# Attention scores in row and column tiles, turns on VectorE and a state softmax that stays in SBUF

## The chip, the cores and the metric

The kernel runs on one core of a Trainium2 chip. The time is that of the device, in microseconds (us), as the median of timed runs. TensorE (PE in the rows) multiplies, with its weight loads shown as PEld; VectorE is DVE, ScalarE ACT, GpSimd POOL. SyncE (SP) issues the transfers.

## The reference

There are 4 batch entries with 8 heads, 512 tokens, 32 states and 64 columns a head. Tokens read the states and states read the tokens, each through a softmax of the same scores; the result, 544 rows for each entry and 512 columns, goes through two feed-forward layers of width 2048.

```python
scores = scale * np.matmul(x, state.transpose(0, 1, 3, 2))
a = softmax(scores)                     # over the 32 states
xread = np.matmul(a, state)
scores2 = scale * np.matmul(state, x.transpose(0, 1, 3, 2))
a2 = softmax(scores2)                   # over the 512 tokens
sread = np.matmul(a2, x)
x = concatenate([xread, sread], axis=2) # tokens to 2176 x 512 rows
h = x @ w_in;  g = elu(h);   x = g @ w_out
h = x @ w_in2; g = mish(h);  out = g @ w_out2
```

(The softmaxes are written out in the reference, with the maximum taken off and 1e-9 added to the sum. The weights arrive as 64-bit floats and are turned into 32-bit ones by the kernel.)

## The kernel before, in words

The token part of the attention is folded into the first layer: since xread is a times the states, xread @ w_in is a times (states @ w_in). `fold` makes those products ("m" tiles, 128 x 512 for four slices of w_in), and `token_reads` makes the probabilities ("x" tiles) for one entry b and one half hf of its heads. The first layer then runs in steps (b, j): a hidden product "h" of 128 slices of w_in by 512 tokens, the activation on ScalarE and VectorE ("e", "g" or "gw"), and the product with a slice of w_out into four PSUM banks ("acc"). The order of the steps is FIRST: entry 0 with j = 0 to 7, entry 1 with j = 0 to 7, entry 0 with 8 to 15, and so on; the states' own rows go through in between, and the second layer follows in five blocks of up to 512 tokens. Steps 0 to 7 of entry 0 use 32-bit products directly ("whole" w_out tiles for the first six); the others are split into a high and a low part, three products each.

`token_reads` loads x (xb), turns it on TensorE (xT), and multiplies it with `sd`, which holds the turned states of one entry in a block-diagonal form: for two token columns of 64 rows each, the states stand in one half and zeros in the other. The scores come out with tokens on the partitions. VectorE takes maximum, difference, sum and product over groups of 32, ScalarE the exponential, and four TensorE turns (pT) bring the probabilities into the form of x1. A copy of the raw scores (raw) goes to DRAM (s2d). `state_reads` fetches them back, and fetches x again in a form with a column of ones; it takes the maximum over the four token columns on VectorE and over the partitions on GpSimd, subtracts, takes the exponential, and multiplies (sr).

Each weight slice is loaded (raw_in, raw_out), decoded by ScalarE (wy) and three VectorE operations (wv, wv, w or whole), and split where the high and low parts are needed. The tiles of w_out take 16 slots called w_out, which also hold early temporaries; those of w_in and m take 16 slots called w_in.

Nothing of the order is left to the run. A planner (`Plan`) is given every operation with its engines, a cost, its due time and the buffers that it needs, and writes each engine's queue; an engine then works its queue strictly in that order. Operations given to either of ScalarE and VectorE are placed by the planner too.

Of the kernel before, what the change touches and what calls it, by code (L numbers as in the profile page):

```python
# [22 lines left out]
P = 128  # L23
# [17 lines left out]
class Buf:  # L41
# [7 lines left out]
    def __getitem__(self, i):  # L49
        return self.t[i]  # L50

# [5 lines left out]
class Plan:  # L57
# [59 lines left out]
    def run(self, take, dma):  # L117

        self.dues(dma)
        free = {}  # L120
# [15 lines left out]
        while todo:  # L136
# [52 lines left out]
            c = op.cost[e] if isinstance(op.cost, dict) else op.cost  # L189
            if e in dma:  # L190
# [25 lines left out]
def attention_elu_mish(  # L216
# [42 lines left out]
    s2d = pools["dram"].tile([P, B, 2, NC, P], F32, name="s2d")  # L259
# [77 lines left out]
    add("DVE", 2.8, make_ident, w=["ident"], due=-50.0)  # L337
# [4 lines left out]
    banks = itertools.cycle(["att", "acc0", "att", "acc1", "h", "acc2", "h"] + ([] if FILL else ["acc3"]))  # L342
    early = True

    def bank(name):
        tag = next(banks) if early else "att"
        return buf("ps", tag, 2 if tag in ("h", "att") else 1, [P, MAXN], F32, name)
# [16 lines left out]
    sd = [pools["at"].tile([P, 2, HH, 2, NS], F32, name=f"sd{b}") for b in range(B)]  # L364
# [11 lines left out]
    def load_states():  # L376
        raw = buf("w", "w_out", NF, [P, 2 * B, 2, D], F32, "st_raw")
        for i in range(2):
            A(ACTQ, 128.0, lambda i=i: nc.scalar.dma_start(
                out=raw[:, :, i, :], in_=state.rearrange("b (g h) n d -> (h n) (b g) d", g=2)),  # L380
              w=[(raw, i)], due=-50.0)
        for b in range(B):
            A("POOL", 0.5, lambda b=b: nc.gpsimd.memset(sd[b], 0.0), w=[("sd", b, i) for i in range(2)], due=-50.0 + b)
        st_raw.append(raw)

    def states(b0, b1):

        raw = st_raw[0]
        if True:
# [8 lines left out]
            for b in range(b0, b1):  # L398
                for i in range(2):
                    r = slice(i * D, (i + 1) * D)  # L400
                    A(EITHER, {"ACT": 0.41, "DVE": 0.43}, lambda e, b=b, b0=b0, i=i, r=r, pt=pt: copy(
                        e, sd[b][r, :, :, i, :],
                        pt[r, (b - b0) * 2 * P:(b - b0 + 1) * 2 * P].rearrange("p (g h n) -> p g h n", g=2, n=NS)),
                        r=[pt], w=[("sd", b, i)])
# [4 lines left out]
    def place_w1(j, k):  # L409
        return w1[j // 2].t.rearrange("p (k f) -> p k f", k=NK)[:, k, j % 2 * P:(j % 2 + 1) * P]  # L410
# [3 lines left out]
    def weight(kind, layer, j, due=None):  # L414
# [45 lines left out]
        if kind == "in" and layer == 1:  # L460
            if j // 2 not in w1:
                w1[j // 2] = buf("w", "w_in", NF, [P, NK * 2 * P], F32, f"w1_{j // 2}_")
            to = w1[j // 2]

            def sign():
                o = to.t.bitcast(U32).rearrange("p (k f) -> p k f", k=NK)[:, :, j % 2 * P:(j % 2 + 1) * P]
# [3 lines left out]
            add("DVE", 0.69, sign, r=[y, v], w=[(to, j % 2)])  # L470
            return
        if layer == 1 and j < WHOLE_OUT:
            w = w_sb["whole", layer, j] = buf("w", f"w_{kind}", NF, [P, DM], F32, f"whole{j}_")
# [12 lines left out]
    after_step = {}  # L486

    def split_weight(kind, layer, j, v):
        w = w_sb[kind, layer, j] = buf("w", f"w_{kind}", NF, [P, 2, DM], F32R, f"w_{kind}{layer}_{j}_")
        add(EITHER, {"ACT": 0.61, "DVE": 0.43}, lambda e: copy(e, w[:, 0, :], v.t), r=[v], w=[(w, 0)])  # L490
        lo, cost = (nc.gpsimd, {"POOL": 1.3}) if (kind, layer, j) in POOL_LO else (nc.vector, {"DVE": 0.69})
        add(next(iter(cost)), cost, lambda: lo.tensor_tensor(
            w[:, 1, :], v.t, w[:, 0, :].bitcast(F32), ALU.subtract), r=[v, (w, 0)], w=[(w, 1)])
# [10 lines left out]
    def m_tile(b, c):  # L504
        if (b, c) not in m_sb:
            m_sb[b, c] = buf("w", "w_in", NF, [P, 2, DM], F32, f"m{b}_{c}_")
        return m_sb[b, c]

    def fold(b, j0, j1):
# [5 lines left out]
        step = min(2, j1 - j0)  # L515

        def f(j):
            w = w1[j // 2].t.rearrange("p (k f) -> p k f", k=NK)
            c = slice(j % 2 * P, (j % 2 + step) * P)
            for k in range(NK):  # L520
                for e in range(2):
                    r, l = slice(e * D, (e + 1) * D), slice(k * NS, (k + 1) * NS)
                    nc.tensor.matmul(pts[e][l, (j - j0) * P:(j - j0 + step) * P], lhsT=sd[b][r, e, k, e, :],  # L523
                                     rhs=w[r, k, c], start=True, stop=True, tile_position=(e * D, k * NS))

        for j in range(j0, j1, step):
            A("PE", 0.1 + mm(4 * step * P), lambda j=j: f(j), w=[(pt, j) for pt in pts], place=[m, *pts],
              lag=FOLD_AHEAD if (b, j0) == (STATES_AFTER[0], STATES_AFTER[1] + 1) else FOLD_LAG,
              r=[("sd", b, 0), ("sd", b, 1)] + [(w1[i // 2], i % 2) for i in range(j, j + step)])
# [19 lines left out]
    x1, own = {}, {}  # L549

    def load_x(b, hf, due=None):

        t = buf("at", "xb", XB, [P, HH, NC, D], F32, "xb")
# [5 lines left out]
        return t  # L559

    def load_x_ones(b, hf):

        t = buf("at", "xb", XB, [P, NC, HH, D + 1], F32, "xb1_")
        A("POOL", 0.1, lambda: nc.gpsimd.memset(t[:, :, :, D:], 1.0), w=[(t, HH)])
        for h in range(HH):
            A(SP, 128.0 * X_WEIGHT, lambda h=h: nc.sync.dma_start(
                out=t[:, :, h, :D],
                in_=x[b, hf * HH + h].rearrange("(p c) d -> p c d", c=NC)), w=[(t, h)], lag=1.0)
        return t

    def token_reads(b, hf):
# [7 lines left out]
        if early and hf:  # L579
            xT = buf("w", "w_out", NF, [P, 2, S], F32, "xT")  # L580
            prr = buf("w", "w_out", NF, [P, 2, NC, P], F32, "prob")
            pr, raw = (lambda: prr[:, 0]), (lambda: prr[:, 1])
            kp, kr = (prr, 0), (prr, 1)
            held = [prr]
        else:
            xT = buf("at", "xT", 1, [P, 2, S], F32)
            kp, kr = buf("at", "prob", 1, [P, NC, P], F32), buf("at", "raw", 1, [P, NC, P], F32)
            pr, raw = (lambda: kp.t), (lambda: kr.t)
            held = [kp, kr]
        mx = buf("at", "mx", 2, [P, NC * HH])  # L590
        sm = buf("at", "sm", 2, [P, NC * HH])
        held += [mx, sm]
        lag = 0.0 if early else 1.0
        ahead = TOKENS_AHEAD[b]
        for q in range(2):
            pt = bank("xT")
# [9 lines left out]
        if b >= TILES_FROM:  # L606

            ps = [bank("scoresT") for t in range(2)]
            sTt = buf("at", "raw", 1, [P, NC, P], F32, "sT")
# [453 lines left out]
```

## Time and profile before

| what | value |
|---|---|
| timed runs, median (lowest, highest) | 753.81 us (752.93, 754.55) |
| profiled execution, first to last instruction (span) | 751.1 us |
| what the median lies above that span | 2.7 us |
| TensorE busy | 732.6 us, 98% |
| VectorE busy | 556.8 us, 74% |
| ScalarE busy | 425.0 us, 57% |
| GpSimd busy | 10.6 us, 1% |
| moved by transfers | 81.71 MB |

The page gives no other time for the profiled execution than its span. The engines run side by side, so their busy times are not to be added; what counts is which of them is never idle, in which stretch, and what ends its waits.

### The profile page before, as it was taken

Reading aid. Unit: us, or ns where it says so; the run is one execution under the profiler, and the core shown is the slowest. Engines: PE = TensorE matmul, PEld = TensorE weight load, DVE = VectorE, ACT = ScalarE, POOL = GpSimd, SP = SyncE. Lnnn points to the kernel's source line nnn. Section 1 sums busy time; section 2 is a strip of 40 time slices with the busy share of each in tenths; the row PEclk is TensorE's granted clock in tenths of the full one; section 3 lists DMA queues with packets and bytes.
Section 4 is the critical chain, followed back from the end, with each engine's and each line's share of the span. In section 5 each row is a group of like instructions: output and inputs, shape, how many; then the busy total and the mean of one; then the engine's idle time right before and its main releaser. Section 6 shows DMA issues by size and latency. Waiting matters only on the chain.

```text
span 751.1 us, 11051 instructions
## 1 busy us (share of the span) xinstructions
PE 732.6 (98%) x4098; PEld 598.0 (80%) x4098; DVE 556.8 (74%) x1048; ACT 425.0 (57%) x759; POOL 10.6 (1%) x27
## 2 busy tenths in 40 slices
PE   5899999999999999999999999999999999999996
PEld 5346677788777879878888888888889999999995
DVE  6988899988689895798999856565567565756564
ACT  3674767655567663577657445454455455545443
POOL 1000000010000000000000000000000000000000
PEclk8899999999999999999999999999999999999999
DMA  9953667453585543665845103000030020001001
GB/s 227 291 154 101 166 161 215 117 169 113 147 256 175 189 140 104 189 196 185 283 162 193 42 1 99 0 1 1 0 99 1 1 83 2 1 1 42 1 1 42
DMA packets 67292, 81.71 MB, mean 109 GB/s; under 512 B 22696, under 2 KB 45992, under 8 KB 67240
## 3 DMA queue, kind: packets, MB, share of 16 engines
q1 hardware_dynamic: 65028, 80.36, 36.1%
q10 hardware_dynamic: 2212, 0.66, 0.4%
q8 instruction: 32, 0.52, 0.3%
q14 instruction: 20, 0.16, 0.1%
HBM read 59.51 MB, written 21.50 MB: 108 GB/s over the span
## 4 chain that ended last, share of the span: by engine, by line
PE 94%; DMA 2%; DVE 1%; ACT 1%; issue 0%; SPq 0%; ACTq 0%
PE acc_acc L849 16%; PE acc_acc L851 15%; PE acc_acc L850 15%; PE h L769 12%; PE h L771 12%; PE h L770 12%; PE fold L523 2%; PE acc_acc L837 2%; PE h L745 2%; PE h L755 2%; DMA raw_in<-in_moe_w_in 2%; PE scores L638 1%; PE pT L663 1%; PE sr L697 1%; DMA xb<-in_x 1%; PE xT L600 1%
## 5 line engine op out<-in xcount | busy, mean ns | idle before, releaser
L788 ACT ACTIVATE e<-h 128x512 f32<-128x512 f32 (+1 forms) x148 | 83.2, 562 | 118.2 <-PE h L771 106.5
L813 ACT CAST g<-e 128x512 fp32r<-128x512 f32 (+1 forms) x142 | 82.4, 581 | 61.9 <-PE acc_acc L851 25.6
L771 PE MATMUL h<-x,w_in 128*128 128x384 f32 (+1 forms) x320 | 114.6, 358 | 0.0
L769 PE MATMUL h<-x,w_in 128*128 128x384 f32 (+1 forms) x320 | 114.4, 358 | 0.0
L770 PE MATMUL h<-x,w_in 128*128 128x384 f32 (+1 forms) x320 | 114.3, 357 | 0.0
L814 DVE TENSOR_TENSOR g<-e,g 128x512 fp32r<-128x512 f32 (+1 forms) x142 | 91.1, 642 | 22.5 <-ACT g L813 21.7
L851 PE MATMUL acc_acc<-w_out,g 128*128 128x512 f32 x272 | 106.9, 393 | 0.0
L850 PE MATMUL acc_acc<-w_out,g 128*128 128x512 f32 x272 | 106.7, 392 | 0.0
L849 PE MATMUL acc_acc<-w_out,g 128*128 128x512 f32 x272 | 105.9, 389 | 0.4 <-ACT g L813 0.4
L849 PE MATMUL acc_acc<-g,w_out 128*128 128x512 f32 x232 | 93.3, 402 | 0.0
L810 DVE TENSOR_TENSOR u<-u,e 128x384 f32<-128x384 f32 (+1 forms) x80 | 48.9, 611 | 57.7 <-ACT e L809 57.6
L850 PE MATMUL acc_acc<-g,w_out 128*128 128x512 f32 x232 | 90.5, 390 | 0.0
L851 PE MATMUL acc_acc<-g,w_out 128*128 128x512 f32 x232 | 90.5, 390 | 0.0
L808 ACT ACTIVATE e<-u,two 128x384 f32<-128x384 f32 (+1 forms) x80 | 52.8, 660 | 50.1 <-DVE u L806 49.9
L805 DVE TENSOR_SCALAR e<-e 128x384 f32<-128x384 f32 (+1 forms) x80 | 30.9, 387 | 48.2 <-ACT e L788 48.1
L769 PEld LDWEIGHTS h<-x,w_in 128*128 128x128 f32 x320 | 60.1, 188 | 7.1
L770 PEld LDWEIGHTS h<-x,w_in 128*128 128x128 f32 x320 | 60.1, 188 | 7.1
L771 PEld LDWEIGHTS h<-x,w_in 128*128 128x128 f32 x320 | 60.1, 188 | 5.0
L851 PEld LDWEIGHTS acc_acc<-w_out,g 128*128 128x128 f32 x272 | 51.0, 187 | 11.0 <-DVE g L814 0.3
L849 PEld LDWEIGHTS acc_acc<-w_out,g 128*128 128x128 f32 x272 | 51.1, 188 | 10.1 <-ACT g L813 0.9
L850 PEld LDWEIGHTS acc_acc<-w_out,g 128*128 128x128 f32 x272 | 51.0, 188 | 9.5
L849 PEld LDWEIGHTS acc_acc<-g,w_out 128*128 128x128 f32 x232 | 43.5, 188 | 13.5 <-issue 3.3
(126 smaller groups left out, 1169.7 us busy)
## 6 DMA issues: line engine op xcount, KB each, us to landing
raw_out<-in_moe_w_out SPq DMA_DIRECT2D x32, 512.0 KB, 4.3
raw_in<-in_moe_w_in SPq DMA_DIRECT2D x32, 256.0 KB, 7.3
raw_in<-in_moe_w_in SPq DMA_DIRECT2D x16, 512.0 KB, 4.2
w2d<-wv SPq DMA_DIRECT2D x32, 256.0 KB, 3.4
xb<-in_x SPq DMA_DIRECT2D x16, 256.0 KB, 4.2
x2d<-o SPq DMA_DIRECT2D x16, 256.0 KB, 2.6
xb<-in_x SPq DMA_DIRECT2D x32, 128.0 KB, 3.9
back_in<-w2d SPq DMA_DIRECT2D x16, 256.0 KB, 3.0
```

What stands on the lines that cost most here:

```text
L769: nc.tensor.matmul(h[:, :n], lhsT=wh, rhs=xh, start=(k == 0), stop=False)
L770: nc.tensor.matmul(h[:, :n], lhsT=wh, rhs=xl, start=False, stop=False)
L771: nc.tensor.matmul(h[:, :n], lhsT=wl, rhs=xh, start=False, stop=(k == nk - 1))
L788: add("ACT", act(n), lambda: nc.scalar.activation(E(), Hh(), AF.Exp), r=[h], w=[e])
L805: add("DVE", 0.1 + 0.00065 * n, lambda: nc.vector.tensor_scalar(E(), E(), E20, None, ALU.min), r=[e], w=[e])
L808: add("ACT", act(n) + 0.12, lambda: nc.scalar.activation(E(), U(), AF.Ln, bias=two), r=[u, "two"], w=[e])
L810: add("DVE", dve(n), lambda: nc.vector.tensor_tensor(U(), U(), E(), ALU.mult), r=[u, e], w=[u])
L813: add("ACT", act(n) + 0.01, lambda: nc.scalar.copy(g[:, 0, :n], E()), r=[e], w=[(g, 0)])
L814: add("DVE", dve(n), lambda: nc.vector.tensor_tensor(g[:, 1, :n], E(), g[:, 0, :n].bitcast(F32), ALU.subtract), r=[e, (g, 0)], w=[(g, 1)])
L849: nc.tensor.matmul(acc.t, lhsT=st[:, 0, :], rhs=mv[:, 0, :], start=fst, stop=False)
L850: nc.tensor.matmul(acc.t, lhsT=st[:, 0, :], rhs=mv[:, 1, :], start=False, stop=False)
L851: nc.tensor.matmul(acc.t, lhsT=st[:, 1, :], rhs=mv[:, 0, :], start=False, stop=lst)
```

## The change

- The scores are made in eight tiles of the TensorE array at once: weights of 64 rows by 32 states (`sd` without its zeros), 256 columns of xT, with the states on the partitions of two PSUM banks. For the first entry VectorE turns them straight from PSUM in blocks of 32 x 32 (two operations of 256 columns) and both banks are copied to raw; for the later ones they are copied first and turned in one operation of 512.
- The softmax over the states then works from SBUF. The probabilities go into x1's form by a second VectorE turn with strided patterns in place of four TensorE turns and a copy. For entries 1 to 3 the split into a high and a low part reads that tile.
- The raw scores stay in SBUF, and so does x. `state_reads` takes the maximum along the free dimension on VectorE, scales it on GpSimd, takes the exponential with its sum on ScalarE, turns the result on TensorE (exT), copies it and multiplies it with the x that was kept. DRAM is not used, and x is not loaded again.
- w_in's first layer is kept in four tiles of 512 columns a row block (w_wide), so that one fold takes 512 columns at a time; the second layer's w_in uses these slots in pairs, and the w_in slots are eight.
- The first entry's x and raw scores lie in three w_out slots until its state reads.
- The state reads start at steps 6, 8, 12, 15, 24, 28, 35 and 38 in place of every fourth from 10 on, and the planner counts other numbers: a start at 0.75 us, TensorE costs times 1.35 up to 16 us, a transfer rate of 245 in place of 330.

```diff
-    sd = [pools["at"].tile([P, 2, HH, 2, NS], F32, name=f"sd{b}") for b in range(B)]
+    sd = [pools["at"].tile([P, 2, HH, NS], F32, name=f"sd{b}") for b in range(B)]
...
-                w1[j // 2] = buf("w", "w_in", NF, [P, NK * 2 * P], F32, f"w1_{j // 2}_")
+                w1[j // NC] = buf("w", "w_wide", NF // NC, [P, NK, NC * P], F32, f"w1_{j // NC}_")
...
-        step = min(2, j1 - j0)
+        step = j1 - j0
...
+        t = buf("w", "w_out", NF, [P, HH, NC, D], F32, "xb0_") if early else \
+            buf("at", "xb", XB, [P, HH, NC, D], F32, "xb")
...
-                    nc.tensor.matmul(
-                        pt.t.rearrange("p (c h n) -> p c h n", c=NC, n=NS)[:, c:c + 2, h, :],
-                        lhsT=xT[:, q, i * P:(i + 1) * P], rhs=sd[b][:, hf, h, :, :], start=True, stop=True)
+                    nc.tensor.matmul(ps[t][l, 0:2 * P], lhsT=sd[b][r, hf, h, :],
+                                     rhs=xT[r, h // 2, h % 2 * 2 * P:(h % 2 + 1) * 2 * P],
+                                     start=True, stop=True, tile_position=(t * D, h * NS))
...
+            if early:
+                A("DVE", 0.43, lambda t=t: nc.vector.transpose(
+                    pr()[:, t * 2 * P:(t + 1) * 2 * P], ps[t][:, 0:2 * P]), r=[ps[t]], w=[(kp, t)])
+            A(EITHER, both(2 * P), lambda e, t=t: copy(e, krv()[:, t, :], ps[t][:, 0:2 * P]), r=[ps[t]], w=[krk(t)],
+              due=T[index[1, b, 0]] - 6.0 if early else None)
+        if not early:
+            A("DVE", 0.69, lambda: nc.vector.transpose(pr(), krv().rearrange("p t f -> p (t f)")),
+              r=[krk(0), krk(1)], w=[(kp, 0), (kp, 1)])
...
-                nc.tensor.transpose(p2[:, c * P:(c + 1) * P], pr()[:, c, :], ident)
+        back = lambda o, i: nc.vector.transpose(
+            o.rearrange("p (c t f) -> p t c f", c=2, t=2), i.rearrange("p (t c f) -> p t c f", t=2, c=2))
         if not b:
-            A(EITHER, both(S), lambda e: copy(e, xt[:, hf, :], p2.t), r=[p2], w=[(xt, hf)], lag=ahead)
+            A("DVE", 0.69, lambda: back(xt[:, hf, :], pr()), r=keys, w=[(xt, hf)], lag=ahead)
...
-        A(SP, 256.0, lambda: nc.sync.dma_start(out=raw.t, in_=s2d[:, b, hf]), r=[("s2d", b, hf)], w=[raw], lag=1.0)
-        A("DVE", 1.04, lambda: nc.vector.tensor_reduce(col.t, turned(), AX.X, ALU.max), r=[raw], w=[col], lag=1.0)
-        A("POOL", 1.2, lambda: nc.gpsimd.partition_all_reduce(tot.t, col.t, P, RMAX), r=[col], w=[tot], lag=1.0)
+        A("DVE", 0.69, lambda: nc.vector.tensor_reduce(
+            top.t, raw().rearrange("p t f -> p (t f)"), AX.X, ALU.max, negate=True),
+          r=rk, w=[top])
+        A("POOL", 0.3, lambda: nc.gpsimd.tensor_scalar(top.t, top.t, SCALE, None, ALU.mult), r=[top], w=[top])
+        A("ACT", 0.8, lambda: nc.scalar.activation(
+            raw(), raw(), AF.Exp, bias=top.t, scale=SCALE, accum_out=den.t), r=[top],
+          w=[*rk, den], lag=1.0)
+                nc.tensor.transpose(pe[:, c * P:(c + 1) * P], raw()[:, c % 2, c // 2 * P:(c // 2 + 1) * P], ident)
...
-GATE_READS, GATE_READS_STEP, GATE_SECOND = 10, 4, 14
-BACKLOG, RATE = 3.0, 330.0
+GATE_READS, GATE_SECOND = (6, 8, 12, 15, 24, 28, 35, 38), 14
+BACKLOG, RATE = 3.0, 245.0
+READY_AT, COLD_UNTIL, COLD = 0.75, 16.0, 1.35
```

What this does to the queues is shown at three places, in the rows of the written order (line, operation, output and inputs, shape, count; the numbers behind the names tell buffers apart). The first is TensorE's queue at the start, before: both halves of x are turned, then all states, then the scores of both halves.

```order
L600 MATMUL xT_137<-ident,xb_104 128x128 x4
L600 MATMUL xT_143<-ident,xb_104 128x128 x4
L600 MATMUL xT_152<-ident,xb_112 128x128 x4
L600 MATMUL xT_159<-ident,xb_112 128x128 x4
L394 MATMUL st_165<-ident,st_raw_102 128x128 x2
L394 MATMUL st_169<-ident,st_raw_102 128x128 x4
L394 MATMUL st_177<-ident,st_raw_102 128x128 x2
L638 MATMUL scores_193<-sd_79,xT_138 128x2x32 x8
L638 MATMUL scores_217<-sd_79,xT_153 128x2x32 x8
```

And with the change (the eight matmuls of a scores group alternate between its two banks):

```order
L614 MATMUL xT_129<-ident,xb_5_103 128x128 x4
L614 MATMUL xT_135<-ident,xb_5_103 128x128 x4
L406 MATMUL st_141<-ident,st_raw_101 128x128 x2
L406 MATMUL st_148<-ident,st_raw_101 128x128 x2
L614 MATMUL xT_152<-ident,xb_16_109 128x128 x4
L626 MATMUL scores_159<-xT_130,sd_78 32x256
L626 MATMUL scores_160<-xT_130,sd_78 32x256
...
L614 MATMUL xT_174<-ident,xb_16_109 128x128 x4
L406 MATMUL st_186<-ident,st_raw_101 128x128 x4
L626 MATMUL scores_196<-xT_153,sd_78 32x256
L626 MATMUL scores_197<-xT_153,sd_78 32x256
```

The first half's scores moved ahead of the fourth turn of x and of half of the states' turns. The second place is VectorE's queue behind those scores, before: the first slice of w_in is decoded (wv, wv, w), and the softmax of the first half follows.

```order
L455 TENSOR_SCALAR wv_190<-wy_182 128x512
L457 SCALAR_TENSOR_TENSOR wv_190<-raw_in_0_25_117,wv_190 128x512
L468 SCALAR_TENSOR_TENSOR w_0_28_209<-wy_182,wv_190 128x4x128
L455 TENSOR_SCALAR wv_215<-wy_203 128x512
L275 COPY raw_195<-scores_193 128x512
L648 TENSOR_REDUCE mx_196<-scores_193 128x16
L649 TENSOR_TENSOR prob_194<-scores_193,mx_196 128x512
L648 TENSOR_REDUCE mx_219<-scores_217 128x16
L649 TENSOR_TENSOR prob_218<-scores_217,mx_219 128x512
```

And with the change:

```order
L633 STREAM_TRANSPOSE prob_161<-scores_159 128x256
L633 STREAM_TRANSPOSE prob_161<-scores_160 128x256
L644 TENSOR_REDUCE mx_163<-prob_161 128x16
L645 TENSOR_TENSOR prob_161<-prob_161,mx_163 128x512
L290 COPY sd_81<-st_186 128x256
L464 TENSOR_SCALAR wv_214<-wy_193 128x512
L466 SCALAR_TENSOR_TENSOR wv_214<-raw_in_0_25_123,wv_214 128x512
L477 SCALAR_TENSOR_TENSOR w_0_28_219<-wy_193,wv_214 128x4x128
L633 STREAM_TRANSPOSE prob_198<-scores_196 128x256
L633 STREAM_TRANSPOSE prob_198<-scores_197 128x256
L644 TENSOR_REDUCE mx_199<-prob_198 128x16
L645 TENSOR_TENSOR prob_198<-prob_198,mx_199 128x512
```

The first half's turns, maximum and difference moved ahead of the first slice's decoding, and four turns came in. The third place is VectorE's queue around the second entry's softmax, where the eighth slice of w_out (w_out_7) gets its low part, before:

```order
L275 CAST w_out_7_84_612<-wv_570 128x512
L545 TENSOR_TENSOR ms_610<-m_0_179_321,ms_610 128x256
L492 TENSOR_TENSOR w_out_7_84_612<-wv_570,w_out_7_84_612 128x512
L655 TENSOR_REDUCE sm_576<-prob_573 128x16
L656 TENSOR_SCALAR sm_576<-sm_576 128x16
L657 RECIPROCAL sm_576<-sm_576 128x16
L658 TENSOR_TENSOR prob_573<-prob_573,sm_576 128x512
L798 SCALAR_TENSOR_TENSOR e_608<-e_608,h_212_567 128x512
L492 TENSOR_TENSOR w_out_1_201_450<-whole_39_409,w_out_1_201_450 128x512
L492 TENSOR_TENSOR w_out_2_206_457<-whole_47_440,w_out_2_206_457 128x512
L814 TENSOR_TENSOR g_636<-e_608,g_636 128x512
```

There g_636 is the activation of step 6. With the change g_604 is that of step 6 and g_648 that of step 7:

```order
L814 TENSOR_TENSOR g_604<-e_568,g_604 128x512
...
L638 STREAM_TRANSPOSE prob_625<-raw_626 128x512
L644 TENSOR_REDUCE mx_627<-prob_625 128x16
L645 TENSOR_TENSOR prob_625<-prob_625,mx_627 128x512
L814 TENSOR_TENSOR g_648<-e_615,g_648 128x512
L509 TENSOR_TENSOR w_out_1_199_410<-whole_39_390,w_out_1_199_410 128x512
L648 TENSOR_REDUCE sm_628<-prob_625 128x16
L649 TENSOR_SCALAR sm_628<-sm_628 128x16
L650 RECIPROCAL sm_628<-sm_628 128x16
L651 TENSOR_TENSOR prob_625<-prob_625,sm_628 128x512
L653 STREAM_TRANSPOSE pT_688<-prob_625 128x2x2x128
L509 TENSOR_TENSOR w_out_7_82_668<-wv_544,w_out_7_82_668 128x512
```

The low part of w_out_7 moved from ahead of step 6's activation to behind step 7's and behind w_out_1's, with a second half's softmax and its two turns between.

## Rows read from the trace of the kernel before

**Rows 1.** The page: busy time of each engine, then TensorE and VectorE by slices.
```profile
PE 732.6 (98%) x4098; PEld 598.0 (80%) x4098; DVE 556.8 (74%) x1048; ACT 425.0 (57%) x759; POOL 10.6 (1%) x27
...
PE   5899999999999999999999999999999999999996
...
DVE  6988899988689895798999856565567565756564
```
**Rows 2.** Waits of TensorE: who waited for whom, us in total, times, longest.
```profile
PE h L769 <- DVE e L798: 1.4, 1, 1.4
...
PE xT L600 <- ACT xT L275: 0.3, 1, 0.3
```
**Rows 3.** Chain that ended last, the start: start us, us, what.
```profile
13.60 0.67 ACT wy L446
...
21.14 1.09 PE pT L663 x4
...
23.32 2.16 PE h L755 x4
...
38.82 3.43 PE acc_acc L837 x8
```
**Rows 4.** Windows: us, busy time of each engine, PEclk, DMA share, GB/s.
```profile
13.75:14.00 0.25, 0.25 (x4) 0.25 (x3) 0.03 (x1) 0.25 (x1) 0.00 (x0) 0.66 1.20 242
24.00:24.25 0.25, 0.25 (x2) 0.21 (x1) 0.25 (x1) 0.25 (x1) 0.00 (x0) 0.86 1.04 262
225.00:250.00 25.00, 25.00 (x168) 19.90 (x168) 23.09 (x46) 17.82 (x31) 1.00 (x1) 1.00 0.54 177
```
**Rows 5.** Chain that ended last, around interludes between the layer's products.
```profile
137.63 0.59 PE fold L523 x16
138.23 0.43 PE acc_acc L849
...
175.75 0.23 PE acc_acc L851
175.98 0.44 PE pT L663 x4
176.42 1.73 PE scores L638 x16
178.15 0.28 PE h L769
...
180.97 1.02 PE fold L523 x32
182.00 0.43 PE acc_acc L849
```
**Rows 6.** Timeline of the start: start us, us, engine, what, idle before it.
```profile
2.88 0.21 DVE L331 STREAM_TRANSPOSE ident_rows<-ident_cols 128x32 f32<-128x32 f32 x1
...
7.28 0.69 DVE L275 COPY xT<-xT 128x512 f32<-128x512 f32 x1 [3.23 <-PE xT L600]
...
11.40 4.85 PE L638 MATMUL scores<-sd,xT 128*128 128x64 f32 x32 [1.04 <-DVE sd L275]
...
11.90 0.43 DVE L455 TENSOR_SCALAR wv<-wy 128x512 uint32<-128x512 uint32 x1 [0.65 <-ACT wy L446]
...
12.36 0.69 DVE L457 SCALAR_TENSOR_TENSOR wv<-raw_in,wv 128x512 uint32<-128x512 uint32 x1
...
15.36 0.68 DVE L648 TENSOR_REDUCE mx<-scores 128x16 f32<-128x512 f32 x1
...
19.39 0.18 DVE L656 TENSOR_SCALAR sm<-sm 128x16 f32<-128x16 f32 x1
19.60 0.25 DVE L657 RECIPROCAL sm<-sm 128x16 f32<-128x16 f32 x1
```
**Rows 7.** Instructions on the tile of the state softmax: duration ns min/median/max, first and last start.
```profile
L685 DVE TENSOR_REDUCE col<-scores x8: 1065/1074/1095, 92.5 to 265.7; 128x128 f32<-128x512 f32 x8
L687 DVE TENSOR_TENSOR scores<-scores,tot x8: 678/686/691, 97.7 to 268.0; 128x512 f32<-128x512 f32 x8
```

More of the change, by code (lines that the diff above doesn't have):

```diff
@@ L50, in __getitem__, with __init__, part @@
         return self.t[i]
+class Half:
+    def __init__(self, base, i):
+        self.base, self.i = base, i
+    def __getitem__(self, i):
+        return self.base.t[:, self.i][i]
+def part(w, i):
+    return (w.base, w.i, i) if isinstance(w, Half) else (w, i)
 class Op:
@@ L398, in states @@
             for b in range(b0, b1):
[L399 to L404, printed above, removed]
+                A(EITHER, both(2 * P), lambda e, b=b, pt=pt: copy(
+                    e, sd[b].rearrange("p g h n -> p (g h n)"), pt[:, (b - b0) * 2 * P:(b - b0 + 1) * 2 * P]),
+                  r=[pt], w=[("sd", b)])
     w1, w_sb, w_back = {}, {}, {}
     def place_w1(j, k):
-        return w1[j // 2].t.rearrange("p (k f) -> p k f", k=NK)[:, k, j % 2 * P:(j % 2 + 1) * P]
+        return w1[j // NC][:, k, j % NC * P:(j % NC + 1) * P]
     loads = itertools.count()
@@ L652, in token_reads, with score_tiles @@
-        A(EITHER, both(S), lambda e: copy(e, raw().rearrange("p c f -> p (c f)"), pt.t), r=all_c, w=[kr],
-          due=T[index[1, b, 0]] + (15.0 if early and LATE else -8.0))
-        A(SP, 256.0, lambda: nc.sync.dma_start(out=s2d[:, b, hf], in_=raw()), r=[kr], w=[("s2d", b, hf)])
-        A("DVE", 0.69, lambda: nc.vector.tensor_reduce(sm.t, prg(), AX.X, ALU.add), r=[kp], w=[sm])
+        ps = [bank("scores", f"acc{2 * hf + t}") for t in range(2)]
+        def score_tiles():
+            for h in range(HH):
+                for t in range(2):
+                    r, l = slice(t * D, (t + 1) * D), slice(h * NS, (h + 1) * NS)
+                    nc.tensor.matmul(ps[t][l, 0:2 * P], lhsT=sd[b][r, hf, h, :],
+                                     rhs=xT[r, h // 2, h % 2 * 2 * P:(h % 2 + 1) * 2 * P],
+                                     start=True, stop=True, tile_position=(t * D, h * NS))
@@ new lines, in token_reads @@
+        A("PE", 0.65, score_tiles, r=[(xT, 0), (xT, 1), ("sd", b)], w=ps, lag=lag, place=held)
+        for t in range(2):
+            if early:
[3 more added lines that the diff above has]
+              due=T[index[1, b, 0]] - 6.0 if early else None)
+        if not early:
+            A("DVE", 0.69, lambda: nc.vector.transpose(pr(), krv().rearrange("p t f -> p (t f)")),
+              r=[krk(0), krk(1)], w=[(kp, 0), (kp, 1)])
@@ L668, in token_reads @@
         else:
[L669 removed]
+            pb = buf("at", "pT", 1, [P, NC, P])
+            A("DVE", 0.69, lambda: back(pb.t.rearrange("p c f -> p (c f)"), pr()), r=keys, w=[pb])
+            A(EITHER, {"ACT": act(S), "DVE": 0.43}, lambda e: copy(
+                e, xt[:, 0, hf, :], pb.t.rearrange("p c f -> p (c f)")), r=[pb], w=[(xt, hf, 0)])
             A("DVE", 0.69, lambda: nc.vector.tensor_tensor(
[L671 to L672 removed]
+                xt[:, 1, hf, :], pb.t.rearrange("p c f -> p (c f)"), xt[:, 0, hf, :].bitcast(F32), ALU.subtract),
+              r=[pb, (xt, hf, 0)], w=[(xt, hf)], lag=ahead)
@@ L1032 @@
 WHOLE_OUT = 6
-X_WEIGHT = 1.5
 POOL_LO = set()
```

179 lines of the change are left out of this document (73 added, 106 removed).

## The prediction

> **What bounds the kernel now.** I read the page's shares and slices first. TensorE is busy 98% of the span, and in the slices it stands at 9 from the third one on, while VectorE stands at 8 to 9 in the first half only [rows 1]. Next the list of TensorE's waits: after the start it waits 1.4 us once, at the hidden product of line 769, and 0.3 us once at an xT turn [rows 2]. So from about 24 us on, time is TensorE's work itself, and an instruction taken off it there is gained in full as long as no new wait comes. Before 24 us it is a chain of VectorE and ScalarE: weight slice landed (13.60), scores, softmax, pT turns at 21.14, hidden product at 23.32 [rows 3]. Last the windows, for VectorE: 23.09 of 25 us busy between 225 and 250 [rows 4], so it has little to give.
>
> **The change part by part.** The profiled span is 751.1 us and the median of the timed runs 753.8; I let those 2.7 us stand and take all terms from the span.
>
> *Scores on TensorE.* The chain prices an interlude by its own piece plus the delay of the piece behind it: scores before, 1.73 + 0.28 - 0.23 (a normal piece) = 1.78 us; one eight-matmul fold of 256 columns, 0.59 + 0.43 - 0.23 = 0.79; a pair of them, 1.02 + 0.43 - 0.23 = 1.22; four turns, 0.44 [rows 5]. The new scores are eight matmuls of 64 x 32 weights over 256 columns, the very form of the 0.79 fold. Six entries (b = 1 to 3, two each) stand in the bound stretch: 6 x (1.78 - 0.79) = **-5.9**.
>
> *Turns.* The pT turns go (6 x 0.45 in that stretch, VectorE takes them over), and the state softmax now turns its exponentials on TensorE, 8 x 0.45, all in that stretch: **+0.9**. The sr products lose one column in 65: nothing.
>
> *Fold 512 wide.* Eight matmuls of 512 columns move what sixteen of 256 move, so 1.22 stays 1.22; I gain only where a pair stood apart (2 x 0.79). Two such pairs lie behind the start (one at 137.63 [rows 5]): 2 x 0.36 = **-0.7**. The third is in the start.
>
> *Start.* VectorE's queue decides. Scores of the first half need xT and one sd copy and can run about 8.5 to 9.3: the first turns end as before, the copy stands at 7.28 [rows 6], sd follows at 8.4. Before, they ran 11.40 to 16.25 for both halves, with long weight loads. From 9.4 VectorE then has, back to back: four score turns of 256 (0.45 each with the gap), two maxima, two subtractions, two sums, two products and two turns back (0.70 each), one sd copy 0.43, two decoded weight slices (0.43 + 0.69 + 0.69 and gaps, 1.85 each) and 0.45 of small ones twice [rows 6]: 1.8 + 7.0 + 0.4 + 3.7 + 0.9 = 13.8, so 23.2. The hidden product's first half can start at 21.2, its second at 23.3; it ends near 24.6 (the rest of the half clock in it) against 25.48 (23.32 + 2.16) [rows 3]. The next part: h(1), 1.72, to 26.3; slices 2 and 3, decoded together, at 26.8; their fold and the second entry's 512-wide one to 28.5; ScalarE's copies behind two weight scalings to 28.9; h(2) to 30.6; output products of step 0 (3.43) to 34.05; half of h(3), a fold, the other half, and the products of step 1: 39.8, with hops 40.1. Before, the same point was 38.82 + 3.43 = 42.25 [rows 3]: **-2.1**. The clock is granted at half (1.2 GHz) from 13.9 to 24.1 us [rows 4], after TensorE had stood idle before 11.40. TensorE is idle at the same times now and resumes at 21.2 (21.14 before), so I let it come back at the same time. A return 2 us later costs 1.0.
>
> *The price of a VectorE turn* is not in the trace at 512 columns. The one turn there is 0.21 us for 32 columns [rows 6]. Taking 0.16 of that as fixed (a 16-column operation takes 0.18 [rows 6]), the rest is at most 1.6 ns a column: 0.98 us for 512. The lower bound is a copy's 0.69 [rows 6]; nothing makes it cheaper. I take 0.69, since 32 columns are mostly fixed cost. The Trainium skill (Vector Engine (DVE) Microarchitecture Reference, section 3.8) says that the turning array sustains one element per cycle and lane; as an estimate with that page's rule that is the lower bound and a sum of 746.4, where the row's upper bound gives 748.7. No run here shows it yet.
>
> *VectorE's balance.* Each token entry gains two turns (about +1.4 us), each state entry loses the 1.07 maximum and the 0.69 subtraction [rows 7] for one 0.69 maximum and, on either engine, an exT copy. Eight of each nearly cancel. What moves is when: from step 0's gw to block 1's first g the order gives VectorE the same work as before (54 us, its operations in the order times these durations), in a stretch where TensorE now wants to be some 3 us faster. There is also a new wait: three w_out slots hold the first entry's x and scores until its state softmax; with x1, six whole and eight split tiles that makes 18 for 16 slots, so w_out_7 finds one only once whole_1 is split, and its low half stands behind step 7's g instead of ahead of step 6's. By the queue it is ready about 8.3 us behind g of step 6; TensorE, which takes up that g 3 us late, arrives 7.7 behind: 0.6 us. Then sr waits for the exT copy, sixth behind x's low half on VectorE (3.8 us, TensorE has 2.6 of work): 1.2, and block 1's first output product 0.3. So 2.1 in place of 1.7 [rows 2]: **+0.4**. Queued behind ScalarE's new exponential (which waits for VectorE's maximum and a one-column GpSimd multiply) are the o copies and block 1's first exponentials; they have some 2 us to spare.
>
> *At nothing:* the planner's new constants and the wide and paired w_in slots (they act only through the order, which I walk), the 16 s2d transfers, 32 padded x loads, the 8 GpSimd reductions (all behind TensorE's work; after 60 us no wait of TensorE names a transfer), the memsets of sd, ScalarE's extra 256-wide copies (its busy share is 57%), and four layer-2 weights decoded later (7 us of VectorE moved behind 275 us, where TensorE needs them 5.5 us apart). Without that cover the last would cost up to its 7.
>
> Sum: -5.9 + 0.9 - 0.7 - 2.1 + 0.4 = **-7.4**; 753.8 - 7.4 = **746.4 us** (a span of 743.7).
>
> **The rivals.**
> *VectorE takes the gain back (0.22).* With 0.98 us turns the start loses 4 x 0.29 = 1.2 and the run from the second entry's scores to w_out_7 another 4 x 0.29, with no slack: 748.7; if the 2.1 us of waits between 60 and 85 us double too, 750.8. For it: 92% busy at 225 to 250 [rows 4]; against it: only 1.7 us of waits before [rows 2]. The Trainium skill (TensorEngine Tiling (Array Packing), PSUM Bottleneck) warns that tiling speeds up the products but not the emptying of PSUM, which may become the limit. That is this case; the trace before agrees only for the one 1.4 us wait.
>
> *More than forecast (0.12).* The new order fits better, no wait stands between 50 and 85 us (-2.1), and the start gains a further 1: 743.3, at best 741.5.
>
> *Nothing left (0.05).* VectorE holds TensorE step by step to 275 us, so that it uses up the 7.4: about 753.8.
>
> *Slower: dear turns (0.05).* Eight 512-column equivalents lie one behind the other on the path (four in the start, four in the 54 to 70 us stretch). The loss is 8 x (turn - 0.69); it eats the gain and 1.5 more at a turn of 1.80 us. At a quarter of a copy's rate (0.16 + 4 x 0.53 = 2.3) it is 12.9: 759.3 (746.4 + 12.9). Only the 0.21 us row stands against it, but for the turns back, with strided patterns, that row says little.
>
> *The tiles do not run side by side (0.01).* Eight matmuls in a row, two passes of 0.21 each, would take 3.4 instead of 0.59 us: 6 x 2.8 = 16.8, so 763.2. The fold of the same form at 0.59 [rows 5] says no.
>
> **How the numbers follow.** The forecast has 0.55, its own range is 744.4 to 748.4 (clock 1.0, hops and waits 1.0 either way). Together 0.55 + 0.22 + 0.12 + 0.05 + 0.05 + 0.01. The range 743.0 to 751.0 leaves out half of "more than forecast", a little of the first rival and the last three: 0.19. 0.2% is 1.5 us, about what a measurement of this kernel tells from none. Faster (below 752.3): 0.55 + 0.12 + 0.21 = 0.88; same 0.06; slower 0.06.
>
> **What would show it.** Scores pieces of 0.59 us with 0.43 behind them, six of them; turns of 512 columns at 0.69 on VectorE; the first hidden product done by 25 and step 1's output products by about 40; eight exT pieces of 0.44; TensorE waits of some 2 us between 60 and 85 and none beyond. Wrong would be: turns near 1 us, a first hidden product later than 24, TensorE waits that name VectorE between 85 and 275 us or in layer 2's first pass, or a clock that stays at half beyond 26 us.

## The result and the profile after

The changed kernel takes **746.5 us** (median of four runs, 745.81 to 747.09), the kernel before 753.6 beside it: a ratio of 0.9905, 95% interval 0.9891 to 0.992, or 7.1 us. The forecast was 746.4. The profiled execution is one of 745.81 us with a span of 743.9, so it stands 1.9 us above its span, and 7.2 us below the span of before.

The page of the changed kernel first, the lines that answer to [rows 1], with the granted clock:

```profile
PE 722.4 (97%) x3874; PEld 579.5 (78%) x3874; DVE 557.6 (75%) x1060; ACT 427.7 (57%) x775; POOL 3.4 (0%) x15
...
PE   4899999999999999999999999999999999999996
...
DVE  6989999887588885789898886565567566666553
...
PEclk8899999999999999999999999999999999999999
```

TensorE is busy 10.2 us less, with 224 matmuls fewer; its idle time grew from 18.5 to 21.5 us. VectorE's work is the same in sum (556.8 and 557.6). The gain is TensorE work taken off, as the forecast had it, and 3.0 us of it went into idle time: summed by windows, TensorE's idle time grew by 3.7 us up to 30 us and fell by 0.7 us between 41 and 275. What it waits for now, the list of its waits says (us in total, times, longest; [rows 2] for before):

```profile
PE h L755 <- DVE x L653: 5.4, 1, 5.4
...
PE fold L540 <- DVE w L477: 3.0, 1, 3.0
PE fold L540 <- ACT m L290: 1.5, 1, 1.5
PE sr L697 <- DVE exT L290: 0.8, 1, 0.8
...
PE xT L614 <- ACT exT L290: 0.2, 1, 0.2
```

The first three of these five lie in the first 29 us. From 41 us to the tail TensorE waits 1.0 us (0.8 for the new exT copy and 0.2) where it waited 1.7. Next the chain that ended last, first around interludes (start us, us, what; the answers to [rows 5]), then in the start ([rows 3]):

```profile
150.94 0.59 PE scores L626 x16
151.53 0.42 PE acc_acc L849
...
181.96 0.44 PE exT L686 x4
...
20.64 2.04 PE h L755 x2
...
23.29 3.14 PE h L755 x6
...
28.15 0.27 ACT m L290
28.42 0.04 issue
28.46 1.36 PE fold L540 x16
...
37.68 3.43 PE acc_acc L837 x8
```

Scores cost 0.59 + 0.42 - 0.23 = 0.78 us, before 1.78; the four turns of the exponentials cost the 0.44 of the pT turns that they replace (two of the eight groups take 0.59 and 0.66 in the chain; they stand right behind sr products, and the product behind them then takes the normal 0.23). The output products of step 1 end at 37.68 + 3.43 = 41.11 us, 1.14 earlier than before. VectorE's turns, grouped by shape (xcount, then busy us and mean ns):

```profile
L653 DVE STREAM_TRANSPOSE pT<-prob 128x512 f32<-128x512 f32 x6 | 4.2, 708 | 0.1
L638 DVE STREAM_TRANSPOSE prob<-raw 128x512 f32<-128x512 f32 x6 | 4.2, 705 | 0.0
...
L633 DVE STREAM_TRANSPOSE prob<-scores 128x256 f32<-128x256 f32 x4 | 1.7, 438 | 0.7 <-ACT raw L290 0.7
...
L653 DVE STREAM_TRANSPOSE x<-prob 128x512 f32<-128x512 f32 x2 | 1.4, 678 | 0.0
```

A turn of 512 columns takes 0.71 us, strided or not: the lower bound of the forecast, hardly above a copy's 0.69 [rows 6]. The 0.7 us of idle time in the third line is new, and comes up below.

### The profile page after: what moved, and what is told of

Read it like the earlier page. It is cut to its first block, busy times and chain, and to the rows that moved or that the text cites. A ratio compares the mean times of both kernels' runs of the same rounds, so it can differ in the third digit from the quotient of the medians.

```text
span 743.9 us, 10519 instructions
## 1 busy us (share of the span) xinstructions
PE 722.4 (97%) x3874; PEld 579.5 (78%) x3874; DVE 557.6 (75%) x1060; ACT 427.7 (57%) x775; POOL 3.4 (0%) x15
## 4 chain that ended last, share of the span: by engine, by line
PE 94%; DVE 3%; DMA 1%; ACT 1%; issue 0%; ACTq 0%
PE acc_acc L849 15%; PE acc_acc L851 15%; PE acc_acc L850 15%; PE h L769 12%; PE h L771 12%; PE h L770 12%; PE acc_acc L837 3%; PE h L755 2%; PE fold L540 2%; PE h L745 2%; DMA st_raw<-in_state 1%; PE xT L614 1%; PE sr L697 1%; PE scores L626 0%; PE acc_att L849 0%; PE acc_att L850 0%
## 5 line engine op out<-in xcount | busy, mean ns | idle before, releaser
L771 PE MATMUL h<-x,w_pair 128*128 128x384 f32 (+1 forms) x160 | 57.3, 358 | 0.0
L771 PE MATMUL h<-x,w_in 128*128 128x384 f32 (+1 forms) x160 | 57.3, 358 | 0.0
L769 PE MATMUL h<-x,w_in 128*128 128x384 f32 (+1 forms) x160 | 57.2, 358 | 0.0
L769 PE MATMUL h<-x,w_pair 128*128 128x384 f32 (+1 forms) x160 | 57.2, 358 | 0.0
L770 PE MATMUL h<-x,w_in 128*128 128x384 f32 (+1 forms) x160 | 57.1, 357 | 0.0
L770 PE MATMUL h<-x,w_pair 128*128 128x384 f32 (+1 forms) x160 | 57.1, 357 | 0.0
```

What stands on the lines that cost most here:

```text
L769: nc.tensor.matmul(h[:, :n], lhsT=wh, rhs=xh, start=(k == 0), stop=False)
L770: nc.tensor.matmul(h[:, :n], lhsT=wh, rhs=xl, start=False, stop=False)
L771: nc.tensor.matmul(h[:, :n], lhsT=wl, rhs=xh, start=False, stop=(k == nk - 1))
```

## The experiments

Every kernel was timed in five rounds beside the kernel before, whose median was 753.4 to 754.0 in all of them.

### What each part gives

**Tiled scores alone**, in the kernel before:

```diff
-TILES_FROM = 4
+TILES_FROM = 1
```

> The kernel before with one constant changed: the scores of entries b = 1 to 3 take the eight-tile form (eight products of 64 x 32 weights over 256 columns), and since the softmax there still stands token by token, four more TensorE turns follow them. Theory (the gain is TensorE's own work in the scores): six entries, each 1.78 to 0.79 us for the products and 0.45 us more for the turns, 6 x 0.54 = 3.2 us off, so about 750.4 us. Rival (the gain of the change comes from the order and from the state softmax, and tiled scores alone are hidden or eaten by the copies behind them): 753 to 754 us.

Measured: 753.86 us, ratio 1.0006 (0.9997 to 1.0015). The rival's number, but not for its reason. The scores do cost 0.79 in this trace, and TensorE's busy time fell by 2.0 us; the idle time grew by 2.4. Its timeline shows one new stall (start us, us, engine, what, idle time before it):

```profile
122.12 1.08 DVE L685 TENSOR_REDUCE col<-scores 128x128 f32<-128x512 f32 x1 [0.59 <-DMA scores<-s2d]
...
123.38 0.73 POOL L686 PARTITION_ALL_REDUCE tot<-col  x1 [6.20 <-DVE col L685]
...
124.99 0.68 DVE L687 TENSOR_TENSOR scores<-scores,tot 128x512 f32<-128x512 f32 x1
...
126.19 0.62 ACT L689 ACTIVATE scores<-scores 128x512 f32<-128x512 f32 x1
...
126.72 0.57 ACT L275 COPY m<-fold 128x512 f32<-128x512 f32 x1
...
127.38 1.10 PE L697 MATMUL sr<-xb,scores 128*32 128x65 f32 x32 [2.24 <-issue]
```

Two things stand in front of the state products. One is their softmax, which runs through a reload, VectorE, GpSimd, VectorE and ScalarE: each of these lines starts behind the one above it, VectorE's subtraction 0.9 us behind, and the exponential ends at 126.81. The other is ScalarE's copy of m out of PSUM. TensorE made that fold just before (124.05 to 125.14), the fold and the state products take their banks from one pool of two, and the copy stands behind the exponential in ScalarE's queue and ends at 127.29. "Issue" is all that the profile says of TensorE's wait; by the times, the copy ended last, 0.1 us before the products started and 0.48 behind the exponential. From 128 to 132 us the granted clock was then 0.66, and the products of that stretch took longer. TensorE came earlier by what the tiles saved, and what it needs next, softmax and bank, could not follow.

**The same, with the state reads let in three steps later:**

```diff
-GATE_READS, GATE_READS_STEP, GATE_SECOND = 10, 4, 14
+GATE_READS, GATE_READS_STEP, GATE_SECOND = 13, 4, 14
```

> The run with the tiled scores alone, with the state reads let in three steps later. Theory (that run's 3.2 us of TensorE work were lost in one stall of 2.2 us at 125 us and the half clock behind it, 128 to 132 us, where the state products waited for the exponential of scores that were reloaded late, a chain through VectorE, GpSimd, VectorE and ScalarE): the stall is gone, 750.0 to 751.5 us. Rival (VectorE holds TensorE there, so a stall of the same size comes elsewhere): 753 to 754 us.

Measured: 750.0 us, ratio 0.9951 (0.9938 to 0.9963): 3.9 us less than the run before, and 3.5 less than the kernel before beside it. The stall is gone (TensorE is busy 16.0 of the 16 us from 120 to 136, at a clock of 1.0). The theory holds in so far as the stall was the loss: tiled scores are worth their 3.2 us of TensorE work, once the state products do not wait. The edit moves the softmax and the fold's banks apart from the products at once, so it does not tell which of the two held them. The late reads without the tiles were not run; the kernel before has no stall in that stretch (16.0 of 16 us busy too) that they could remove.

**The planner's constants of before**, in the changed kernel (besides these four, the latency of a transfer, 2.0 in place of 2.2, and the cost of making the identity, 2.8 in place of 3.2):

```diff
-BACKLOG, RATE = 3.0, 245.0
-READY_AT, COLD_UNTIL, COLD = 0.75, 16.0, 1.35
+BACKLOG, RATE = 3.0, 330.0
+READY_AT, COLD_UNTIL, COLD = 0.0, 0.0, 1.0
...
```

> The changed kernel with the planner's five constants of before (start of the engines at 0, no dearer TensorE at the start, transfer rate 330, latency 2.0, identity cost 2.8). Only the order moves: at the start all turns of x and of the states stand ahead of both scores, and the second entry's first fold stands later. Theory (the constants act only through the order of the start; the bound stretch does not care): no change from the changed kernel, or up to 1.5 us lost in the start, 746.5 to 748.0 us. Rival (the gain hangs on the new order): 750 us or more.

Measured: 752.13 us, ratio 0.9984 (0.9976 to 0.9993). The rival: 5.6 of the 7.1 us hang on these six numbers. Timeline of this kernel:

```profile
33.57 1.79 PE L614 MATMUL xT<-ident,xb 128*128 128x128 f32 x8 [4.92 <-DMA xb<-in_x]
```

A planner that takes transfers to be faster than they are puts the second entry's x turns ahead of step 0's output products, and TensorE stands 4.9 us in front of a transfer that is under way. In the changed kernel the same turns stand at 52.04 us and wait for nothing. The forecast let the constants act through the order alone, which is what happened; it walked the new order, and so has them in its sum.

**These constants in the kernel before:**

```diff
-        free = {}
+        free = dict.fromkeys(("PE", "DVE", "ACT", "POOL", *dma), READY_AT)
...
+            if e == "PE" and t < COLD_UNTIL:
+                c *= COLD
...
-BACKLOG, RATE = 3.0, 330.0
+BACKLOG, RATE = 3.0, 245.0
+READY_AT, COLD_UNTIL, COLD = 0.75, 16.0, 1.35
```

> The kernel before with the five planner constants of the changed kernel (engines ready at 0.75, dearer TensorE at the start, transfer rate 245, latency 2.2, identity cost 3.2); nothing else. Theory (the constants are worth 5.6 us to the changed kernel only because without them its order has a stall of 4.9 us for x's transfer, which the kernel before has not): 753 to 755 us, no change. Rival (a planner that knows the start better gains by itself): 748 to 751 us.

Measured: 752.92 us, ratio 0.9991 (0.9982 to 0.9999). The theory: about half a microsecond, and by the interval 0.1 to 1.4. The constants are hardly a gain by themselves; they keep the new kernel's order from a stall that the old one did not have.

**The fold 256 wide again**, in the changed kernel:

```diff
-        step = j1 - j0
+        step = min(2, j1 - j0)
```

> The changed kernel with the fold of w_in issued 256 columns at a time (two groups of eight products in place of one, 3840 bytes less to stream in neither). Theory (a fold costs by its columns: 16 products of 256 took 1.22 us before and 8 of 512 take 1.22 us after): 746 to 747.5 us, with only pairs that the order sets apart losing 0.36 us each. Rival (fewer, wider products are themselves a gain of some 0.3 us in each of about 15 folds): 750 to 751 us.

Measured: 749.52 us, ratio 0.9944 (0.9932 to 0.9957): 3.0 us slower than the changed kernel, between the two. (The remark on bytes in what was expected says nothing and can be passed over.) Where two groups stand together they cost 1.22 us in this trace too, so width itself gives nothing. Three pairs stood apart, as here in its chain:

```profile
118.05 0.59 PE fold L540 x16
118.64 0.43 PE acc_acc L849
...
120.23 0.59 PE fold L540 x16
120.82 0.43 PE h L769
```

Each such pair costs 2 x 0.79 = 1.58 in place of 1.22: 1.1 us for three. Another 1.5 us came in the start, where step 0's output products waited 2.1 us for their weights, so that step 1's started at 39.02 in place of 37.52 us (timelines). That is 2.6 of the 3.0 us; the rest is not accounted for. A wide instruction is worth what its being one piece saves: the order cannot tear it apart.

### Which engine binds, and until when

**Every score product twice:**

```diff
-            for h in range(HH):
+            for h in [*range(HH), *range(HH)]:
```

> The changed kernel with every score product issued twice (16 in place of 8, same output). Theory (TensorE is the bound in blocks 0 to 3, so its work there shows in full): the second eight stream for 0.43 us and share the switch, 6 x 0.43 = 2.6 us, up to 8 x 0.43 = 3.5 with the two in the start: 749.1 to 750.0 us. Rival (VectorE holds TensorE step by step, so that TensorE's work is hidden): 746.5 us, no change.

Measured: 749.17 us, ratio 0.9945 (0.9932 to 0.9957): 2.7 us on top of 746.5. The theory: a piece of 1.02 us stands where 0.59 stood, 0.43 us more, and six of them are 2.6. TensorE's work in blocks 0 to 3 is time.

**VectorE's turns twice**, in entries 1 to 3:

```diff
+            for _ in range(2):
                 A("DVE", 0.69, lambda: nc.vector.transpose(pr(), krv()...
...
+            for _ in range(2):
                 A("DVE", 0.69, lambda: back(pb.t...
```

> The changed kernel with each of VectorE's 512-column turns of entries b = 1 to 3 issued twice, 12 turns of 0.70 us more on VectorE (8.4 us), same output. Theory (TensorE is the bound and VectorE has slack except where TensorE already waits for it, at 69 to 77 us): between none and 3 us lost, 746.5 to 749.5 us. Rival (VectorE is as close to the bound as TensorE through the token entries, so that its work shows in full): 753 to 755 us.

Measured: 751.52 us, ratio 0.9969 (0.9957 to 0.998): 5.0 us slower, 2 more than the theory allowed and less than the rival's 6.5. It is lost in one stretch. I count the third product of the split hidden steps (L771, and L773 there) through both timelines. The first and the 13th, in the changed kernel and then with the turns:

```profile
66.13 0.40 PE L771 MATMUL h<-x,ms 128*128 128x512 f32 x1
...
95.85 0.39 PE L771 MATMUL h<-x,ms 128*128 128x512 f32 x1
```

```profile
67.78 0.39 PE L773 MATMUL h<-x,ms 128*128 128x512 f32 x1
...
101.39 0.39 PE L773 MATMUL h<-x,ms 128*128 128x512 f32 x1
```

The 21st starts at 113.43 and 118.97, the 85th at 271.02 and 277.37. Of the 5.54 us at the 13th, 1.24 are there before any doubled turn: step 1's output products start at 37.52 and 38.76 us, in an execution whose half clock lasted to 25.9 in place of 24.0 us. So the four extra turns of the second entry (2.8 us) cost 4.3 us, and the eight of the third and fourth entries (5.6 us) 0.8, which together fit the 5.0 us of the medians. TensorE's waits of that kernel, 60 to 130 us:

```profile
PE h L771 <- ACT x L290: 2.3, 1, 2.3
PE sr L699 <- ACT xT L290: 1.0, 1, 1.0
PE h L772 <- DVE x L664: 0.5, 1, 0.5
PE xT L614 <- ACT exT L290: 0.2, 1, 0.2
```

The hidden products of block 1 wait for x, and the granted clock is 0.87 in the stretch from 72 to 85 us, which makes the loss larger than the work. Through the second entry's softmax (its turns end by 75 us) VectorE has nothing to spare; at the third and fourth entries' (155 us on) TensorE binds; between them no turn stands, and nothing was tested. The Trainium skill (TensorEngine Tiling (Array Packing), PSUM Bottleneck) warns that what empties PSUM may become the limit. The engine that does part of this here, VectorE, is short at the second entry, by the 4.3 us, and not at the later two, by the 0.8; but the doubled turns read SBUF, so no run here tests the emptying itself.

### The start

**The second entry's first fold let in two steps later:**

```diff
-                begin(max(0, index[1, b, c * NC] - GATE_M), fold, b, ...
+                begin(max(2, index[1, b, c * NC] - GATE_M), fold, b, ...
```

> The changed kernel with one gate moved: the second entry's first fold may begin only with step 2, so it no longer stands right behind the first entry's third fold, whose two PSUM banks it takes. Theory (the wait of 1.46 us at 28.46 us is for ScalarE's copies out of those banks, and it is on the path): 1.0 to 1.5 us faster than the changed kernel, 745.0 to 745.5 us. Rival (the next thing, the whole w_out slice that step 0's output products need, is as late, as the 2.1 us wait for it in the run with the 256-wide fold suggests): 746.5 to 747.5 us.

Measured: 747.11 us, ratio 0.9911 (0.9897 to 0.9924). The rival's number. The wait stays as it is and changes its owner:

```profile
PE h L755 <- ACT m L290: 1.5, 1, 1.5
```

I had read the 1.46 us as a wait for two PSUM banks. It is a wait for the same two ScalarE copies, but step 2's hidden product needs their output just as early. ScalarE makes them at 28.06 in the changed kernel, behind two weight scalings.

**The raw scores copied behind VectorE's turns**, on ScalarE:

```diff
         for t in range(2):
-            A(EITHER, ... copy(e, krv()[:, t, :], ps[t]...)
+            A("ACT" if early else EITHER, ... copy(e, krv()[:, t, :], ps[t]...), after=turned)
```

> The changed kernel with the order of two readers swapped: in the first entry ScalarE copies the raw scores out of PSUM only after both of VectorE's turns of them. Theory (VectorE's second turn waited 0.71 us at 10.35 us for ScalarE's copy out of the same bank, and VectorE is the chain of the start): x turned 0.6 to 0.7 us earlier, 745.8 us, at best 745.5. Rival (the start hangs on the weight slices that land, or on a later wait): 746.5 us, no change.

Measured: 746.44 us, ratio 0.9903 (0.9889 to 0.9916): no change. The first half of the theory holds in part: the two turns now run as one piece of 0.78 us, and x is there for TensorE at 20.31 in place of 20.64, half of what was expected. But step 1's output products end at 38.10 + 3.43 = 41.53, later than 41.11: the clock (by windows of 1 us), which is full again at 24.0 us in the changed kernel's profiled execution, was so at 25.1 in this one, and the six products that took 3.14 took 3.87. In the trace of the fold let in later, whose program is the same up to 23 us, it was 25.8. The moment moves by almost 2 us between executions.

**TensorE kept busy**: 58 identity turns that nobody reads.

```diff
+    def keep(n):
+        turns(pools["ps"].tile([P, MAXN], F32, tag="h", bufs=2, name="keep"), n)
...
+            if (b, j0) == (0, 0):
+                keep(KEEP[1])      # behind the first fold, 36
...
+            if xt is x1[0] and hf:
+                keep(KEEP[0])      # behind the last scores of entry 0, 22
```

> The changed kernel with 58 more identity turns on TensorE that nobody reads, 22 behind the first entry's last scores and 36 behind its first fold, where TensorE waits for the weights and for x; the order of everything else is that of the changed kernel. Theory (the clock is granted at half from about 14 to 24 or 26 us because TensorE stands idle before, and the half clock costs the hidden products of steps 0 and 1 some 2 us): the clock stays at 1.0 from 14 us on, the first hidden product takes 1.1 in place of 2.05 us, and the start ends 0.5 to 1.5 us earlier, what ScalarE's copies leave of it: 745.0 to 746.0 us, with executions closer together. Rival (the start is VectorE's and ScalarE's chain, and the half clock is hidden under it): 746.5 us with the clock at 1.0.

Measured: 746.78 us, ratio 0.991 (0.9896 to 0.9924). The clock was 1.0 up to 22 us and the first hidden product took 1.10 us in place of 2.04, so that half held; but from 22.6 to 26 us the clock was at half once more, step 1's output products ended at 38.64 + 3.43 = 42.07, later than 41.11, and the time did not change.

**Both edits together:**

> The changed kernel with the 58 turns and with the raw scores copied behind VectorE's turns, together. Theory (the earlier x of 0.3 to 0.8 us was lost to the half clock, which ended at 25.9 us there): the two add, 744.3 to 745.5 us. Rival (ScalarE's copies of the third fold, 28 to 29 us, end both): as the run with the 58 turns alone.

Measured: 746.81 us, ratio 0.9909 (0.9896 to 0.9923). This is the run that settles the start. Its window from 13 to 24 us (the changed kernel's clock is 0.53 there):

```profile
13.00:24.00 11.00, 9.39 (x80) 5.98 (x78) 10.86 (x24) 5.27 (x13) 0.00 (x0) 1.00 1.12 247
```

The clock never fell. Its timeline behind step 1:

```profile
38.95 1.88 PE L764 MATMUL h<-x,m 128*128 128x512 f32 x4
...
44.59 1.13 PE L764 MATMUL h<-x,m 128*128 128x512 f32 x2 [0.33 <-DVE gw L804]
...
53.35 0.62 ACT L290 CAST w_out<-wv 128x512 fp32r<-128x512 f32 x1 [1.08 <-DVE w_out L512]
...
53.87 0.58 ACT L290 COPY xT<-xT 128x512 f32<-128x512 f32 x1
...
54.50 1.06 PE L631 MATMUL scores<-xT,sd 64*32 64x256 f32 x16 [1.11 <-ACT xT L290]
```

The products behind step 1's start at 38.95, where they start at 40.95 in the changed kernel: 2.0 us gained. At the first split step all of it is gone (its third product starts at 66.55, and at 66.13 there), although TensorE, VectorE and ScalarE work in the same order between. TensorE waits 0.33 for a gw, then 1.11 for an xT copy that ScalarE makes late because it waited 1.08 for a VectorE operation. VectorE is busy 18.11 of the 19 us from 41 to 60 (17.27 in the changed kernel). What the start gives, VectorE takes back before 66 us. No version here beats the changed kernel by more than the spread of its runs.

**GpSimd's fills put back**, eight of 128 x 256:

```diff
+    for b in range(B):
+        for _ in range(2):
+            A("POOL", 0.3, lambda b=b: nc.gpsimd.memset(sd[b], 0.0), ...)
```

> The changed kernel with eight GpSimd memsets of the four sd tiles (128 x 256 each) put back at the start, which the copies overwrite. Theory (VectorE's five small additions for the identity took 0.45 us each before while GpSimd filled memory, and 0.17 after, where it did not): the additions go back to 0.3 to 0.45 us, the identity is ready 0.5 to 1 us later, and the time stays within 0.5 us of the changed kernel, since the start then waits for the state transfer that lands at 7.3 us. Rival (the small additions were slow for another reason): additions of 0.17 us as in the changed kernel.

Measured: 746.7 us, ratio 0.9906 (0.9893 to 0.992): no change in time; the additions slow down, by less than expected (last section).

## Why the prediction was right

*Bound and scores.* Right as put: 6 x (1.78 - 0.79); the run with the products doubled shows that TensorE's time there is the kernel's. What I did not see is that this part needs another one. Alone it gave nothing, because the state products could not follow; I had taken the state part as a cost (turns, +0.9), and its new place and form are also a cover of the -5.9. In the changed kernel that softmax starts from a copy in the core's own memory, and TensorE's one wait for it is 0.8 us. Which of the two does it, place or form, is not shown: the late reads show that the place is enough for the tiles alone, and no run has the whole change with the old softmax.

*Turns.* TensorE's +0.9 holds, 0.44 to 0.45 each where no sr product stands ahead. VectorE's price is 0.71, close to the 0.69 taken. The Trainium skill (Vector Engine (DVE) Microarchitecture Reference, section 3.8) has one element per cycle and lane for the turning array; by that rule the lower bound held, and the trace agrees.

*Fold.* -0.7 for the two pairs that stand apart in the old order. In the new order the 256-wide fold would stand apart three times, 1.1 us, so against that order the term is a little under-sized.

*Start.* Mis-sized: -2.1 forecast, -1.14 in the profiled execution, and in others less. The step that failed is "their fold and the second entry's 512-wide one to 28.5": I let both folds run when their weights were decoded, with ScalarE's copies of the first behind them, at 28.9. The second fold takes the banks that these copies empty, so it runs behind them, from 28.46 to 29.82 in place of an end at 28.5. It could not simply be moved away: the copies end at 28.7, and the run with the fold let in later shows that step 2 needs them as early as the second fold does. The clock's half level was set to end as before, and it did (24.0); that its end moves between executions I had no row for. Nor is the term worth its size: the run that started 2.0 us better was no faster.

*Waits.* +0.4 forecast, -0.7 measured (1.0 us in place of 1.7): the wait for w_out_7 did not come (why was not followed), the one for exT came with 0.8 instead of 1.2. This error and that of the start are of one size and cancel, so that the forecast met the measured time to 0.1 us is luck; the terms themselves are off by about 1 us each.

With these sizes (the start by the profiled execution) the sum is -5.9 + 0.9 - 0.7 - 1.1 - 0.7 = -7.5, and the spans differ by 7.2.

*The rivals.* "VectorE takes the gain back" did not happen to the sum, but its mechanism is real and its place was right, from the start through the second entry's softmax: it holds back what the start gains, and by the run with the turns doubled a dearer turn would have cost more than its own time (4.3 us for 2.8). Dear turns and tiles one behind the other are excluded by the rows above. "More than forecast" was half right, the waits fell, and the start did not gain more. "Nothing left" is near to what the planner's old numbers make of it (752.1), but by a wait for a transfer and not through VectorE; I gave the constants no rival of their own, since the order was there to be read.

## What to carry to other kernels

When work is taken off the engine that binds, ask at each place what it will reach sooner and whether that can be ready: here the same tiles gave nothing or 3.5 us, by the place of the state products. An edit that seems to be a cost can be the cover of another's gain, so take parts out one at a time before you credit one. And a gain in the start counts only if the next stretch has slack on every engine; the engine that waits there for nothing need not be the one that binds.

## What the runs showed of the hardware

Small VectorE operations slow down while GpSimd fills memory. The five additions that build the identity (1 to 16 columns), duration ns min/median/max:

In the changed kernel, without fills:

```profile
L344 DVE TENSOR_SCALAR ident_cols<-ident_cols x5: 154/170/174, 0.9 to 1.7; 128x1 f32<-128x1 f32 x1, 128x2 f32<-128x2 f32 x1, 128x4 f32<-128x4 f32 x1, 128x8 f32<-128x8 f32 x1
```

With eight fills of 128 x 256, 0.32 us each:

```profile
L344 DVE TENSOR_SCALAR ident_cols<-ident_cols x5: 154/240/242, 0.9 to 1.9; 128x1 f32<-128x1 f32 x1, 128x2 f32<-128x2 f32 x1, 128x4 f32<-128x4 f32 x1, 128x8 f32<-128x8 f32 x1
```

In the kernel before, with four fills of 128 x 512 of 0.54 us each, the median was 452 ns and the longest 455. So in both kernels with fills an addition takes about as long as one fill, less 0.08 or 0.09 us. Why is open; the columns do not decide it (in the kernel before 4, 8 and 16 columns take 452 to 455 ns; the first addition, of one column, takes 154 in all three kernels), and it cost nothing here, since the start waits for the state transfer, which lands at 7.3 us.

When the clock falls behind the same idle time is not the same in each execution. TensorE stands idle from 11.5 us on in the traces of the changed kernel's order; the clock fell there between 13.7 and 15.8 us, and was full again between 24.0 and 26.0. With TensorE kept busy it fell at 22.6 us in one execution and not at all in the other.
